# First weights split just before the first expert slot, and routing steps moved into the pauses of the slots

## The chip, the cores and the metric

The kernel runs on one core of a Trainium2 chip. Time is the device time of one execution in microseconds (us), median of several runs. The engines are TensorE (PE), VectorE (DVE), ScalarE (ACT), GpSimd (POOL) and SyncE (SP), which here only starts transfers. Each engine works through its own list of instructions in order; an instruction that waits for another engine or for a transfer holds up everything behind it in its list. PEld is the load of a stationary operand.

## The reference, cut to what matters

An attention over 32 memory rows per head, followed by a mixture of experts in which every token takes the one expert with the largest logit. Shapes: batch 8, heads 8, 576 positions of 64; so 4608 tokens of 512; 8 experts of 512 x 1024 and 1024 x 512. Everything is float32.

```python
a = softmax(phi, axis=2)                       # over the positions
k_m = einsum('bhsm,bhsd->bhmd', a, k)          # 32 memory rows per head
v_m = einsum('bhsm,bhsd->bhmd', a, v)
attn = softmax(q @ k_m.T / 8) @ v_m            # x: 4608 tokens of 512
logits = x @ w_gate;  e = argmax(logits)       # one expert per token
gate = softmax(logits)[e];  eom = sigmoid(x @ w_output_gate)[e]
out[token] = gate * eom * (relu(x[token] @ w1[e]) @ w2[e])
```

## The kernel before

**Attention.** The eight batches go in four pairs (`bp`), each pair in five units of queries, so 20 turns `t`, and three more turns until the last unit is through. One turn walks through the list `ORDER` of 16 letters; a letter's `LAG` says which unit it handles in turn `t`, unit `t - LAG`: `C` the scores, `S` shift by the maximum, `X` exponent on ACT, `D` divide, `B` transpose back, `V0` and `V1` the product with the memory values and its copy to `xo`, which is then stored to the table `xs` in DRAM. `M` and `m` advance the memory rows of later pairs. The instructions of each engine stand in the order in which this Python code emits them.

**Routing.** When a pair's last unit is stored, `rank(bp)` picks each token's expert from the logits, counts tokens per expert with matmuls against ones and a triangle (L246, L879 to L883, into the one bank `pr`), writes the gate values to `xs` and builds one-hot masks `Aw` on POOL. Beside it run the lists: `route_early(0)` after pair 1 makes list a (slots 0 and 1), `route_early(1)` after pair 2 list b (slots 2 to 4), `route_late` after pair 3 list l (all others). A list is a table of token numbers, made by a chain of small DVE operations and one group of matmuls (L227); `known` says that the experts of its slots are decided, `listed` that the token numbers are there. All of this is in generators that are advanced a few steps at a time, by the letters `R0`, `R1`, `R4` in the attention's turns.

**Expert slots.** A slot is up to 384 tokens (three blocks of 128) of one expert. POOL gathers the rows (`xg`, three buffers from turn 19 on), PE turns them (L991), ACT and DVE split them into a high and a low part (`xh`, `xl`), and three matmuls stand for one product of full precision. A slot's weights come in eight chunks `u`: SP loads a chunk (`w`, L508), ACT casts its high part (L519), DVE subtracts for the low part (L520). Chunks 0 to 3 give the hidden layer in groups of 12 matmuls of 384 columns (L1124), with `hh` on ACT and `hl` on DVE; chunks 4 to 7 give the output (L1143, 512 columns), which ACT scales and POOL scatters to `out`. The rows of the next slot are turned during chunks 4 to 7. There are 14 fixed slots and 22 spare ones behind branches.

**The seam.** Turns up to `t` = 19 (`START`), letter `S`, run alone; then slot 0 begins, and what is left of the attention is advanced in pauses of the slots: `hook()` is called 20 times in a slot of three blocks, after every group of 12 matmuls in chunks 0 to 3 and after every block in chunks 4 to 7. `hold(n)` lets a generator wait until `clock` has moved by `n` (by one at each letter of the attention, or at each pause once that is done); `take_pr()` waits until the bank `pr` has been read. `LATE` holds these numbers: `pe` ahead of routing matmuls, `dve` between them and their reader, `w` ahead of the first weight load, `lg` for the sum of the logits.

The lines on which the steps rest:

```python
elif w == "W":
    if order[0]["known"] and stream.parted < ring.size:
        stream.split(ring.size)
...
def hook():
    gathers(i)
    clock[0] += not att.gens
    (att if att.gens else late).step(HOOK[min(i, 5)])
```

`ring` (split chunks) has two buffers, four from turn 19 on; `raw` (loaded chunks) three, then five.

Of the kernel before, what the change touches and what calls it, by code (L numbers as in the profile page):

```python
# [19 lines left out]
NBP = B // 2  # L20
# [15 lines left out]
ORDER = ["R4", "W", "X", "S", "R0", "m", "D", "M", "B", "V0", "R1", "R1", "V1", "M", "m", "C"]  # L36
LAG = {"X": 1, "B": 2, "D": 1, "V": 3, "C": -1}
TICK = 0
HOOK = (2, 2, 2, 2, 2, 2)
START = 19  # L40
NKV = 8
NQ = 3
# [7 lines left out]
NPK = 1  # L50
PHI1 = 6
NEA = 3
LATE = {"lg": 8, "w": 2, "pe": 0, "dve": 0}
GROW = ((2, 2, 2), (6, 1, 0))
PUMP = (2, 1)
TURN = {3: (1, 4, 6, 9), 2: (1, 2, 4, 5)}
LAST = 1
# [8 lines left out]
def attention_moe(tc, phiT, kv, qT, wgo, wall, out):  # L66
# [3 lines left out]
    with contextlib.ExitStack() as ctx:  # L70
# [134 lines left out]
        def table(nm, q, nch, nblk):  # L205

            while nm == "l" and "rl" not in env:
                yield
            bw = (env["rl"] if nm == "l" else rt).tile([P, nch, 2, nblk], BF16, name="bw" + nm)
            w = min(nch, 9 * NBL // nblk // 9 * 9)  # L210
            for c in range(0, nch, w):
                b3 = [P, w, nblk]
                eq = rt.tile([P, 9 * NBL], BF16, name="eq")
                eq = eq[:, 0:w * nblk].rearrange("p (c b) -> p c b", c=w)
                V.tensor_tensor(eq, iota_blk[:, 0:nblk].unsqueeze(1).to_broadcast(b3),
                                q[:, c:c + w].unsqueeze(2).to_broadcast(b3), ALU.is_equal)
                yield
                for i in range(2):
                    V.tensor_tensor(bw[:, c:c + w, i], eq,
                                    tok_hl[:, i, c:c + w].unsqueeze(2).to_broadcast(b3), ALU.mult)  # L220
                yield
            yield
            yield from hold(LATE["pe"])
            yield from take_pr()
            pi = ps_r.tile([P, 2, NBL], F32, name="pr")
            for c in range(nch):
                T.matmul(pi[:, :, 0:nblk], Aw[:, c], bw[:, c], start=(c == 0), stop=(c == nch - 1))  # L227
            yield
            yield from hold(LATE["dve"])
            iv = rt.tile([P, NBL], F32, name="iv")  # L230
            i2 = rt.tile([P, NBL], F32, name="i2")
            ivv, i2v = iv[:, 0:nblk], i2[:, 0:nblk]
            V.tensor_copy(i2v, pi[:, 1, 0:nblk])
            yield
            V.scalar_tensor_tensor(ivv, pi[:, 0, 0:nblk], 64.0, i2v, ALU.mult, ALU.add)  # L235
            taken.clear()
            yield
            ig, io = idx[nm]
            V.tensor_scalar(ig[:], ivv, 1.0, 0.0, ALU.subtract, ALU.max)
            V.tensor_scalar(i2v, ivv, 0.0, 100000.0, ALU.is_equal, ALU.mult)  # L240
            yield
            V.scalar_tensor_tensor(io[:], ivv, -1.0, i2v, ALU.add, ALU.add)  # L242
# [6 lines left out]
        def route_early(k):  # L249

            nm, n, s0, nch = "ab"[k], NPS[k], sum(NPS[:k]), (k + 2) * NCH
            eo, en = epcs[k], epcs[k + 1]
            yield from hold(LATE["pe"])
            yield from take_pr()
            n_ = counts(k + 1)
            yield
            yield from hold(LATE["dve"])
            fi = rt.tile([P, 1, E], F32, name="fi")
            ge = triples(fi[:, 0], n_, thr_e)
            next(ge)  # L260
            taken.clear()
            yield
            yield from ge
            V.scalar_tensor_tensor(fi[:, 0], fi[:, 0], 3.0, eo[:], ALU.mult, ALU.subtract)
            yield
            inc = (yield from prefix(fi[:], 1))[:, 0]
            exc = rt.tile([P, E], F32, name="exc")
            ie = rt.tile([P, E], F32, name="ie")
            V.tensor_scalar(ie[:], inc, 3.0 * n, None, ALU.min)
            V.tensor_tensor(exc[:], inc, fi[:, 0], ALU.subtract)  # L270
            yield
            V.tensor_scalar(exc[:], exc[:], 3.0 * n, None, ALU.min)
            cle = count_le(slot[:, s0:s0 + n], iota_3[:, 0:n], n, ie[:])
            next(cle)
            yield
            next(cle)
            V.tensor_tensor(ie[:], ie[:], exc[:], ALU.subtract)
            yield
            last(cle)
            V.tensor_tensor(en[:], eo[:], ie[:], ALU.add)  # L280
            V.tensor_tensor(exc[:], exc[:], eo[:], ALU.subtract)
            known(*order[s0:s0 + n])
            yield
            if k == 0:
                yield from hold(LATE["w"])
                stream.fetch()
            t1, t2, t3 = yield from lookup(nch, exc[:], en[:], eo[:])
            while k + 1 not in ranked:
                yield
            j = jg[:, 0:nch]  # L290
            V.scalar_tensor_tensor(t1, t1, 1.0, j, ALU.add, ALU.add)
            V.tensor_tensor(t2, j, t2, ALU.is_lt)
            V.tensor_tensor(t3, j, t3, ALU.is_ge)
            yield
            V.tensor_tensor(t1, t1, t2, ALU.mult)
            yield
            V.tensor_tensor(t1, t1, t3, ALU.mult)
            yield
            yield from table(nm, t1, nch, 3 * n)
            for z in order[s0:s0 + n]:  # L300
                z["listed"] = True
            if k == 0:
                gathers(0)
            yield

        def route_late():
            yield from hold(LATE["pe"])
            yield from take_pr()
            n_ = counts(NBP - 1)
            yield  # L310
            yield from hold(LATE["dve"])
# [107 lines left out]
        env = {}  # L419
# [4 lines left out]
        def take_pr():  # L424

            while taken:
                yield
            taken.append(1)

        def hold(n):  # L430

            end = clock[0] + n
            while clock[0] < end:
                yield
# [23 lines left out]
        ring = Ring([P, 2, 1024], F32R, "whl")  # L458
# [16 lines left out]
        order = slots  # L475
# [354 lines left out]
        def rank(bp, lg):  # L830
# [41 lines left out]
            yield  # L872

            def rest():
                yield from hold(LATE["pe"])
                yield from take_pr()

                pr = ps_r.tile([P, NCH, E], F32, name="pr")
                T.matmul(pr[:], strict[:], oh, start=True, stop=False)  # L879
# [135 lines left out]
        def attention():  # L1015
# [8 lines left out]
            for t in range(NT + LAG["V"]):  # L1024
                for w in ORDER:
# [2 lines left out]
                        if w == "M" or t % 5 < 4:  # L1028
                            mem.step()
                    elif w[0] == "R":  # L1030
                        rou.step(int(w[1:]))
                    elif w == "W":
                        if order[0]["known"] and stream.parted < ring.size:
                            stream.split(ring.size)
                    elif w == "W":

                        while t == NT - 1 and stream.split(2):
# [175 lines left out]
        def run(st):  # L1213
# [8 lines left out]
            def hook():  # L1222
                gathers(i)
                clock[0] += not att.gens
                (att if att.gens else late).step(HOOK[min(i, 5)])

            for i in range(lo, hi):
                gathers(i, i + 1)
# [10 lines left out]
                    several(i, st, nxt, hook)  # L1239
                else:  # L1240
                    single(i, st, nxt)
                if i == LAST:
                    settle()

        pso.close()
        pso = contextlib.ExitStack()
        env["pd"] = pso.enter_context(tc.tile_pool(name="pd1", bufs=1, space=PSUM, reuse_waits="tile"))
        env["ps"] = pso.enter_context(tc.tile_pool(name="p0", bufs=5 - NPK, space=PSUM, reuse_waits="tile"))
        n = NPE + NPT + NPP
        run(stream)  # L1250
        used = nc.values_load(slot[0:1, NSLOT:], min_val=0, max_val=NSS)  # L1251
# [48 lines left out]
```

## Time and profile before

| | us |
|---|---|
| median of 3 runs (lowest, highest) | 617.65 (616.18, 618.13) |
| the profiled execution, its own time | 618.26 |
| its span in the trace | 616.6 |
| PE busy in the span | 541.8 (88%) |
| DVE, ACT, POOL busy | 344.2, 273.2, 160.1 |

Matmuls overlap, so a busy PE means that its list does not stand still. A timeline row gives start and length in us, engine, line and operation, output and inputs, shape and count, and in square brackets how long the engine stood idle before it and what ended that. A row of waits gives the total in us, how often, and the longest. A row of the windows view gives the stretch, its length, and for each of PE, PEld, DVE, ACT and POOL the busy time and the count, then PE's clock, the share of the transfers and GB/s.

### The profile page before, as it was taken

Reading aid. Unit: us, or ns where it says so; the run is one execution under the profiler, and the core shown is the slowest. Engines: PE = TensorE matmul, PEld = TensorE weight load, DVE = VectorE, ACT = ScalarE, POOL = GpSimd, SP = SyncE. Lnnn points to the kernel's source line nnn. Section 1 sums busy time; section 2 is a strip of 40 time slices with the busy share of each in tenths; the row PEclk is TensorE's granted clock in tenths of the full one; section 3 lists DMA queues with packets and bytes.
Section 4 is the critical chain, followed back from the end, with each engine's and each line's share of the span. In section 5 each row is a group of like instructions: output and inputs, shape, how many; then the busy total and the mean of one; then the engine's idle time right before and its main releaser. Section 6 shows DMA issues by size and latency. Waiting matters only on the chain. (4 is left out here: it accounts for less than half of the span.)

```text
span 616.6 us, 10779 instructions
## 1 busy us (share of the span) xinstructions
PE 541.8 (88%) x4107; PEld 467.0 (76%) x4107; DVE 344.2 (56%) x686; ACT 273.2 (44%) x456; POOL 160.1 (26%) x192
## 2 busy tenths in 40 slices
PE   4688777349999599989999999999999999999990
PEld 2355555239889489888998989898998989989970
DVE  3487989585655269975452635444453536556300
ACT  4475654424444146434444435344444436455310
POOL 2244466252410437012211303030201203210100
PEclk9779879659999799989999999999999999999995
DMA  8999999674555647855463755455554647673000
GB/s 305 412 368 389 406 366 335 224 231 126 170 164 167 204 110 258 312 168 161 153 195 120 228 154 195 137 173 175 158 175 133 193 154 227 200 238 114 27 5 25
DMA packets 41276, 124.13 MB, mean 201 GB/s; under 512 B 9408, under 2 KB 9472, under 8 KB 40832
## 3 DMA queue, kind: packets, MB, share of 16 engines
q1 hardware_dynamic: 35136, 102.71, 50.7%
q0 software_dynamic: 6080, 20.65, 9.5%
q8 instruction: 34, 0.56, 0.4%
q14 instruction: 26, 0.21, 0.1%
HBM read 102.99 MB, written 20.87 MB: 201 GB/s over the span
## 5 line engine op out<-in xcount | busy, mean ns | idle before, releaser
L1124 PE MATMUL bps<-xh,whl 128*128 128x384 f32 (+1 forms) x896 | 214.1, 322 | 0.0
L1143 PE MATMUL bps<-whl,hh 128*128 128x512 f32 x608 | 204.2, 401 | 0.0
L520 DVE TENSOR_TENSOR whl<-w,whl 128x1024 fp32r<-128x1024 f32 x112 | 137.0, 1230 | 76.3 <-ACT whl L519 76.2
L1124 PEld LDWEIGHTS bps<-xh,whl 128*128 128x128 f32 x896 | 157.2, 190 | 1.1 <-issue 0.2
L1124 PE MATMUL bps<-xl,whl 128*128 128x384 f32 (+1 forms) x448 | 143.9, 321 | 0.0
L1143 PEld LDWEIGHTS bps<-whl,hh 128*128 128x128 f32 x608 | 115.0, 189 | 23.4
L519 ACT CAST whl<-w 128x1024 fp32r<-128x1024 f32 x112 | 116.2, 1045 | 10.1 <-DMA w<-wall 8.1
L1143 PE MATMUL bps<-whl,hl 128*128 128x512 f32 x304 | 119.2, 392 | 0.0
L1129 ACT ACTIVATE hh<-bps 128x384 fp32r<-128x384 f32 (+1 forms) x96 | 48.9, 509 | 109.1 <-PE bps L1124 109.1
L1130 DVE SCALAR_TENSOR_TENSOR hl<-bps,hh 128x384 fp32r<-128x384 f32 (+1 forms) x96 | 55.4, 577 | 68.1 <-ACT hh L1129 68.0
L1124 PEld LDWEIGHTS bps<-xl,whl 128*128 128x128 f32 x448 | 85.3, 190 | 0.5
L1104 POOL DMA_INDIRECT out<-y,idx_ol x23 | 24.2, 1053 | 212.0 <-ACT y L1103 183.5
L993 DVE TENSOR_TENSOR xl<-bps,xh 128x384 fp32r<-128x384 f32 (+1 forms) x48 | 27.8, 578 | 69.1 <-ACT xh L992 68.9
L1143 PEld LDWEIGHTS bps<-whl,hl 128*128 128x128 f32 x304 | 57.7, 190 | 10.4
L992 ACT CAST xh<-bps 128x384 fp32r<-128x384 f32 (+1 forms) x48 | 23.8, 496 | 77.6 <-PE bps L991 77.6
L1103 ACT ACTIVATE y<-bps,xg 128x512 f32<-128x512 f32 x38 | 26.2, 688 | 66.5 <-PE bps L1143 23.7
L991 PE MATMUL bps<-ident,xg 128*128 128x128 f32 x152 | 26.2, 289 | 8.4 <-DMA xg<-xs,idx_gb 6.5
L481 POOL DMA_INDIRECT xg<-xs,idx_gl x23 | 28.2, 1226 | 20.9 <-DVE idx_ol L242 14.1
L826 PE MATMUL bpd<-ve_b,aT 64*128 64x144 f32 (+1 forms) x320 | 29.8, 340 | 3.6 <-DVE iv L235 2.3
L828 ACT COPY xo<-bpd 128x576 f32<-128x576 f32 x36 | 22.3, 638 | 22.1 <-PE bpd L826 9.4
L991 PEld LDWEIGHTS bps<-ident,xg 128*128 128x128 f32 x152 | 20.4, 148 | 15.3 <-issue 6.7
L793 POOL TENSOR_TENSOR ea<-ea,mx 128x512 f32<-128x512 f32 (+1 forms) x20 | 19.2, 959 | 48.6 <-DVE mx L791 48.6
(232 smaller groups left out, 435.5 us busy)
## 6 DMA issues: line engine op xcount, KB each, us to landing
w<-wall SPq DMA_DIRECT2D x112, 512.0 KB, 3.6
kvt<-kv SPq DMA_DIRECT2D x32, 512.0 KB, 8.2
xs<-xo SPq DMA_DIRECT2D x16, 576.0 KB, 5.5
qt<-qT SPq DMA_DIRECT2D x16, 512.0 KB, 9.1
ph<-phiT SPq DMA_DIRECT2D x3, 1152.0 KB, 12.5
kv<-kv SPq DMA_DIRECT2D x4, 512.0 KB, 10.4
ph<-phiT SPq DMA_DIRECT2D x4, 288.0 KB, 3.7
xs<-xo SPq DMA_DIRECT2D x8, 144.0 KB, 3.9
```

The costliest lines, as they stand in the source:

```text
L481: G.indirect_dma_start(out=z["xg"][:, k], out_offset=None, in_=xs[0:z["rows"]], in_offset=bass.IndirectOffsetOnAxis(ap=z["idx"][0][:, q:q ...
L519: A.copy(hl[:, 0], w[:])
L520: V.tensor_tensor(hl[:, 1], w[:], hl[:, 0].bitcast(F32), ALU.subtract)
L826: T.matmul(px[to:to + n, r, sl], z["aT"][h, o:o + n], ves[2 * bp + b][h, g], start=True, stop=True)
L991: T.transpose(pt[:, j, k * P:(k + 1) * P], xg[:, k, o:o + P], ident[:])
L993: V.tensor_tensor(xl[:, c:c + w, 0:n], pt[:, :, 0:n], xh[:, c:c + w, 0:n].bitcast(F32), ALU.subtract)
L1103: A.activation(y[:], py, AF.Copy, scale=z["xg"][:, k, P:P + 1])
L1104: G.indirect_dma_start(out=out, out_offset=bass.IndirectOffsetOnAxis(ap=z["idx"][1][:, z["q0"] + k:z["q0"] + k + 1], axis=0), in_=y[:], in ...
L1124: T.matmul(pb[:, j % pb.shape[1], 0:n_], w[:, b, o:o + P], x[a][:, cc, 0:n_], start=(n == 0), stop=(n == 11))
L1129: A.activation(h_[:, js, 0:n_], pb[:, :, 0:n_], AF.Relu)
L1130: V.scalar_tensor_tensor(l_[:, js, 0:n_], pb[:, :, 0:n_], 0.0, h_[:, js, 0:n_].bitcast(F32), ALU.max, ALU.subtract)
L1143: T.matmul(py[k], h[u - 4][a][:, f, k * P:(k + 1) * P], w[:, b, DM * f:DM * f + DM], start=(u == 4 and f == 0 and n == 0), stop=(u == 7 an ...
```

## The change

Four edits. The letter `W` no longer splits a chunk as soon as slot 0's expert is known; its second branch, so far never reached, now splits two chunks in turn 19, just ahead of slot 0. The letters `R` do nothing once three pairs have been stored, so that the third pair's `rank` and `route_early(1)` do not start before slot 0. In every pause of a slot the attention takes three letters where it took two, and the routing takes two steps of its own. `hold` waits only once the slots have begun (`env["open"]`), with `pe` 3 and `dve` 2 in place of 0 and 0, and stands behind `take_pr()`, where it stood ahead of it. `settle()`, which frees the attention's memory for more weight buffers, may come after the first slot if the attention is done by then; the order of the built program shows it after slot 1, as before.

```diff
-HOOK = (2, 2, 2, 2, 2, 2)
+HOOK = (3, 2)
...
-LATE = {"lg": 8, "w": 2, "pe": 0, "dve": 0}
+LATE = {"lg": 8, "w": 2, "pe": 3, "dve": 2}
...
             yield
+            yield from take_pr()
             yield from hold(LATE["pe"])
-            yield from take_pr()
             pi = ps_r.tile([P, 2, NBL], F32, name="pr")
...
         def hold(n):
 
+            if "open" not in env:
+                return
             end = clock[0] + n
...
                     elif w[0] == "R":
-                        rou.step(int(w[1:]))
-                    elif w == "W":
-                        if order[0]["known"] and stream.parted < ring.size:
-                            stream.split(ring.size)
+
+                        if len(left) < NBP - 1:
+                            rou.step(int(w[1:]))
                     elif w == "W":
 
                         while t == NT - 1 and stream.split(2):
                             pass
...
                 clock[0] += not att.gens
-                (att if att.gens else late).step(HOOK[min(i, 5)])
+                att.step(HOOK[0])
+                (rou if rou.gens else late).step(HOOK[1])
...
-                if i == LAST:
+                if "hs" not in env and (i == LAST or not att.gens):
                     settle()
...
+        env["open"] = True
         n = NPE + NPT + NPP
         run(stream)
```

The same exchange of `take_pr` and `hold` is made in `route_early`, `route_late` and `rank`. In the changed kernel lines behind L432 stand two to three numbers higher.

**ACT, where slot 0's expert becomes known** (`whl` is a split chunk, `ea` the scores, `kvm` the memory rows, `kT` and `vT_b` their transposes). Before:

```order
L797 ACTIVATE ea<-ea 128x256
L828 COPY xo<-bpd 128x576 x2
L519 CAST whl<-w 128x1024
L797 ACTIVATE ea<-ea 128x512
L706 ACTIVATE kvm<-pk,rs 128x128 x2
L720 COPY kT_198<-bpa 64x128 x2
L721 COPY vT_b<-bpa 64x256
```

Now:

```order
L799 ACTIVATE ea<-ea 128x256
L830 COPY xo<-bpd 128x576 x2
L799 ACTIVATE ea<-ea 128x512
L708 ACTIVATE kvm<-pk,rs 128x128 x2
L722 COPY kT_198<-bpa 64x128 x2
L723 COPY vT_b<-bpa 64x256
```

The first cast is gone from here, and with it the first subtraction from DVE; both stand, with a second chunk, directly ahead of slot 0. On SP the slot number is read, and three chunks are loaded, ahead of the store of `xo` and the load of queries behind which they stood.

**DVE, the last instructions ahead of slot 0** (`ohg`, `oc`, `ohc`, `zs`, `gd` belong to the third `rank`, `tge` and `fi` to list b, `xl` to slot 0's rows). Before:

```order
L813 STREAM_TRANSPOSE aT<-ea 128x512
L861 TENSOR_TENSOR ohg<-desc,pm 128x72
L863 TENSOR_REDUCE oc<-ohg 128x8
L864 TENSOR_TENSOR w__1909<-ohg,lg 128x72
L868 TENSOR_TENSOR ohc_90<-ohc_89,oc 128x8
L871 TENSOR_REDUCE zs<-w__1909 128x9
L184 TENSOR_TENSOR tge<-pr,thr_e 128x104
L186 TENSOR_REDUCE fi<-tge 128x8
L885 TENSOR_REDUCE gd<-w__1908 128x9
L520 TENSOR_TENSOR whl<-w,whl 128x1024
L788 STREAM_TRANSPOSE ea<-bpd 128x256
```

Now:

```order
L815 STREAM_TRANSPOSE aT<-ea 128x512
L522 TENSOR_TENSOR whl<-w,whl 128x1024 x2
L790 STREAM_TRANSPOSE ea<-bpd 128x256
L793 TENSOR_REDUCE mx<-ea 128x8
L947 TENSOR_REDUCE lg<-xo 128x32
L995 TENSOR_TENSOR xl<-bps,xh 128x384 x4
```

The steps of the third rank, and PE's counting matmuls L246 to L883 with them, have moved into slot 0, where L246 now stands between two groups of 12 expert matmuls and L881 (L879 before) two groups later; two subtractions stand where one stood.

**DVE, the end of list b** (`idx_gb` and `idx_ob` are its token numbers, `hl` a group of slot 1's hidden layer). Before, the rows at the end of that layer, with the turned rows of slot 2 (`xl`) behind them:

```order
L1130 SCALAR_TENSOR_TENSOR hl<-bps,hh 128x384 x2
L520 TENSOR_TENSOR whl<-w,whl 128x1024
L239 TENSOR_SCALAR idx_gb<-iv 128x9
L240 TENSOR_SCALAR i_2573<-iv 128x9
L242 SCALAR_TENSOR_TENSOR idx_ob<-iv,i_2573 128x9
L993 TENSOR_TENSOR xl<-bps,xh 128x384
```

Now, at the end of slot 0, with the first `hl` of slot 1 behind them:

```order
L995 TENSOR_TENSOR xl<-bps,xh 128x384
L239 TENSOR_SCALAR idx_gb<-iv 128x9
L240 TENSOR_SCALAR i_2489<-iv 128x9
L242 SCALAR_TENSOR_TENSOR idx_ob<-iv,i_2489 128x9
L522 TENSOR_TENSOR whl<-w,whl 128x1024
L1131 SCALAR_TENSOR_TENSOR hl<-bps,hh 128x384
```

List b stands a whole hidden layer (eight groups of 12 matmuls) earlier against the matmuls of slot 1.

More of the change, by code (lines that the diff above doesn't have):

```diff
@@ L252, in route_early @@
             eo, en = epcs[k], epcs[k + 1]
+            yield from take_pr()
             yield from hold(LATE["pe"])
-            yield from take_pr()
             n_ = counts(k + 1)
@@ L306, in route_late @@
         def route_late():
+            yield from take_pr()
             yield from hold(LATE["pe"])
-            yield from take_pr()
             n_ = counts(NBP - 1)
@@ L874, in rest @@
             def rest():
+                yield from take_pr()
                 yield from hold(LATE["pe"])
-                yield from take_pr()
                 pr = ps_r.tile([P, NCH, E], F32, name="pr")
```

## The prediction

> **What bounds the kernel now.** I read the page's forty slices first, then all waits of TensorE (PE), then the timelines of the engines around the longest ones.
>
> ```profile
> PE   4688777349999599989999999999999999999990
> ```
>
> From slice 9 on PE is full, except for the 5 in slice 13. Slices 7 and 8, about 108 to 139 us, are nearly empty: there attention ends and the expert slots begin. So time is to be had only before slot 0 starts and in that one later hole. The longest waits of PE in the whole span that the change can touch (us in total, times, longest):
>
> ```profile
> PE bpa L715 <- ACT kvm L706: 13.0, 3, 9.2
> PE bps L991 <- DMA xg<-xs,idx_gb: 6.5, 3, 6.0
> PE pr L227 <- DVE bwl L219: 2.3, 2, 1.5
> ```
>
> The 9.2 is one stall of PE, seen on PE and then on ScalarE (ACT):
>
> ```profile
> 115.55 0.73 PE L715 MATMUL bpa<-ident,kvm 128*128 128x128 f32 x2 [9.16 <-ACT kvm L706]
> ```
> ```profile
> 105.03 1.18 ACT L828 COPY xo<-bpd 128x576 f32<-128x576 f32 x2 [3.27 <-DMA xs<-xo]
> 113.66 1.04 ACT L519 CAST whl<-w 128x1024 fp32r<-128x1024 f32 x1 [7.45 <-DMA w<-wall]
> 114.61 0.62 ACT L797 ACTIVATE ea<-ea 128x512 f32<-128x512 f32 x1
> ```
>
> ACT is free at 106.21, but its next instruction is the cast of the first weights, whose transfer is still under way. The softmax exponent and the copies of kvm, whose data were there, stand behind it. PE's order then waits for ACT.
>
> **The lead-in, term by term.** The change takes this cast, and the next two, out of the attention turns. With it gone the exponent (L797) can start when POOL has its input ready:
>
> ```profile
> 105.62 1.04 POOL L793 TENSOR_TENSOR ea<-ea,mx 128x512 f32<-128x512 f32 x1
> ```
>
> That is at 106.7, 7.9 us earlier than 114.61. VectorE (DVE) gains less:
>
> ```profile
> 109.06 0.18 DVE L295 TENSOR_TENSOR q<-q,q 128x18 f32<-128x18 f32 x1
> 115.88 0.71 DVE L788 STREAM_TRANSPOSE ea<-bpd 128x512 f32<-128x512 f32 x1
> 121.48 1.22 DVE L520 TENSOR_TENSOR whl<-w,whl 128x1024 fp32r<-128x1024 f32 x1
> 126.22 0.56 DVE L239 TENSOR_SCALAR idx_ga<-iv 128x6 int32<-128x6 f32 x1
> 127.05 0.23 DVE L852 TENSOR_REDUCE lm<-lg 128x9 f32<-128x72 f32 x1
> 130.43 0.65 DVE L813 STREAM_TRANSPOSE aT<-ea 128x512 f32<-128x512 f32 x1
> 131.01 2.37 DVE L861 TENSOR_TENSOR ohg<-desc,pm 128x72 bf16<-128x72 f32 x1
> 135.30 1.23 DVE L520 TENSOR_TENSOR whl<-w,whl 128x1024 fp32r<-128x1024 f32 x1 [0.44 <-ACT whl L519]
> 136.44 0.44 DVE L788 STREAM_TRANSPOSE ea<-bpd 128x256 f32<-128x256 f32 x1
> ```
>
> After L295 ends at 109.24 DVE has one more small step (L297, 0.13) and then the transpose of 115.88: at 109.4, so 6.5 us earlier. From there DVE's own work sets the pace. The subtraction at 121.48 goes (1.1 to the next start): 7.6. The four rank steps that fill 127.05 to 128.00 go: 8.6. Then, from 131.01 to 136.44, DVE spends 5.4 us on the next rank steps and one subtraction; now two subtractions of 1.15 each stand there, 2.3, which by itself makes 11.7. But these two need their casts, and the casts stand on ACT behind the last two copies of xo:
>
> ```profile
> 128.30 1.33 PE L826 MATMUL bpd<-ve_b,aT 64*128 64x144 f32 x8 [0.78 <-ACT xo L828]
> 133.96 0.17 PE L246 MATMUL pr<-ohc,ones_b 128*128 128x8 bf16 x1 [3.72 <-DVE ohc L868]
> 136.94 2.82 PE L991 MATMUL bps<-ident,xg 128*128 128x128 f32 x12 [1.93 <-DVE ea L788]
> ```
> ```profile
> 131.31 0.26 ACT L865 ACTIVATE w__1908<-w__1908 128x72 f32<-128x72 f32 x1 [3.06 <-POOL w__1908 L855]
> 131.48 0.62 ACT L828 COPY xo<-bpd 128x576 f32<-128x576 f32 x1
> ```
>
> The copy at 131.48 waited for the rank exponent before it, not for PE, which was done at 129.63. Without that exponent it ends at 130.3 in the old count; that chain runs 7.7 to 7.9 earlier, so at 122.5. Two casts of 1.0 end at 124.5, the second subtraction at 126.0, the short transpose at 126.5, and slot 0's transposes (old start 136.94, 0.06 behind that transpose) begin at 126.6: **−10.3**. The gathered rows must be there too:
>
> ```profile
> 127.07 1.25 POOL L481 DMA_INDIRECT xg<-xs,idx_ga  x1 [0.32 <-DMA xs<-xo]
> 201.23 1.05 POOL L481 DMA_INDIRECT xg<-xs,idx_gb  x1 [17.14 <-DVE idx_ob L242]
> ```
>
> List a (L239, 126.22) moves up by 7.6, so the gather goes out at about 119.3. For slot 2 PE had all three blocks 7.1 us after the first issue (201.23, third block at 208.33, quoted below): 126.4. Both estimates agree. Bounds: −6.5, if nothing but the shift of 115.88 survives, and −11.7 by DVE alone.
>
> **The later hole.** PE's timeline:
>
> ```profile
> 200.53 0.39 PE L1143 MATMUL bps<-whl,hh 128*128 128x512 f32 x1
> 206.94 0.45 PE L991 MATMUL bps<-ident,xg 128*128 128x128 f32 x1 [6.03 <-DMA xg<-xs,idx_gb]
> 208.33 0.47 PE L991 MATMUL bps<-ident,xg 128*128 128x128 f32 x1 [0.27 <-DMA xg<-xs,idx_gb]
> 208.46 0.78 PE L1143 MATMUL bps<-whl,hh 128*128 128x512 f32 x1
> 211.86 0.63 PE L1143 MATMUL bps<-whl,hh 128*128 128x512 f32 x2
> 213.94 0.39 PE L1143 MATMUL bps<-whl,hh 128*128 128x512 f32 x1
> 214.17 0.49 PE L991 MATMUL bps<-ident,xg 128*128 128x128 f32 x3
> 214.41 0.47 PE L1143 MATMUL bps<-whl,hh 128*128 128x512 f32 x1
> ```
>
> List b ends on DVE only at 201, its gather goes out at 201.23, and slot 2's transposes, in slot 1's second half, stand waiting. Nine matmuls from 211.86 to 213.94 give a pitch of 0.231. Without the hole three transposes (0.24, from 214.17 to 214.41) would follow 200.53 + 0.23 and the next matmul would stand at 201.0, not at 208.46: 7.45. The 18 matmuls from 208.46 to 214.17 took 5.71 instead of 18 × 0.231 = 4.16, since PE's clock was down after the stop: 1.55. Together 9.0. In the change list b ends on DVE before slot 1's first hl, eight groups of 2.08 us (the length of one is shown below) ahead of its use, and the gather needs some 7. The whole hole goes: **−9.0**. Bounds: 0, if the list is late again, and −9.0.
>
> List l's matmuls waited 2.3 us for bwl just after its last product was made. They now stand three pauses, half a weight chunk of PE work each, behind it: **−2.0**, between 0 and −2.3.
>
> **What is added.** The counting matmuls of the third rank (L246 to L883, 0.17 + about 0.5 beside 133.96) stood in idle time and now stand in slot 0: **+0.9** with their weight loads. In slot 0 PE also waits for DVE at them:
>
> ```profile
> 142.04 0.49 ACT L1129 ACTIVATE hh<-bps 128x384 fp32r<-128x384 f32 x1 [1.76 <-PE bps L1124]
> 144.12 0.49 ACT L1129 ACTIVATE hh<-bps 128x384 fp32r<-128x384 f32 x1 [1.59 <-PE bps L1124]
> ```
> ```profile
> 134.16 0.27 DVE L184 TENSOR_TENSOR tge<-pr,thr_e 128x104 f32<-128x104 f32 x1
> ```
>
> Twelve expert matmuls take 2.08 us (142.04 to 144.12). L881 reuses the bank that L184 reads, one such group after L246's pause. But between the group's end and L184 stand hh (0.49), a cast (1.04), a subtraction (1.23), a reduction and L184 (0.27): some 3.5, so PE waits 1.4. Behind the waiting L881 stand only expert matmuls. At L246 the same count (two casts and two subtractions fall in the first pause) gives 1.0, and the copies of xo behind casts 0.4: **+2.8**. Bounds: 0, if DVE catches up, and 8. DVE was busy
>
> ```profile
> 137.00:179.00 42.00, 42.00 (x234) 36.70 (x235) 27.09 (x72) 19.04 (x31) 12.39 (x16) 0.96 0.56 169
> ```
>
> 27 of 42 us there (third busy number), and takes over about 9 us of rank and list steps: 36 of some 45, so it is late at single places and no bound of the slot. The transfer of the first weights costs nothing: the first was in at 113.66, later ones at most a few us after it, and slot 0 now starts at 126.6.
>
> **Sum:** −10.3 − 9.0 − 2.0 + 0.9 + 2.8 = −17.6. The profiled execution took 618.26 (span 616.6), 0.6 above the median of 617.65; it gives 600.7, and against the median **600 us**. PE is full from the hole to the end of the last fixed slot, so what is gained there reaches the end.
>
> **Rivals.**
>
> *A store takes the cast's place.* SyncE now reads the slot and issues three weight loads ahead of the store of 106.23, which goes out 3 us later:
>
> ```profile
> 95.20 0.38 SPq L937 DMA_DIRECT2D xs<-xo  x1
> ...
> 106.23 0.36 SPq L937 DMA_DIRECT2D xs<-xo  x1
> ```
>
> The copy of xo two turns on needs that buffer. If the store took as long as the one that ACT waited for at 105.03 (issued 95.20: 9.8 us), it would land at 119.3, while the copy would be ready at 115.3: 4 us lost on ACT and PE alike, 604. With 3 more of stalls in slot 0 it is 607. For it: three weight loads of 512 KB now go out just ahead of the store. Against: the wait at 105.03 is ACT's only one of its kind between 90 and 140 us. Chance 0.18.
>
> *The hole stays.* Ranking the third pair starts later than before, so list b could come late and slot 2 wait again: 600 + 9 = 609. Against it stands DVE's order. Chance 0.08.
>
> *DVE pays for POOL, and slots 0 and 1 stall: slower.* POOL's masks now stand beside the expert work of both slots:
>
> ```profile
> L911 POOL TENSOR_SCALAR Aw<-iota_row,row 128x128 bf16<-128x128 bf16 x18 | 15.6, 880 | 9.1 <-DVE row L901 9.0
> ```
>
> If DVE stood still during all 18 masks and PE with it, that is 15.6 us, and with the upper bound of the stalls (5.2 more) 621. It decides once DVE's slack in slot 0, 45 − 36 = 9, is used up. Against: these 18 ran in expert slots before too, where PE never waited for hl. [...] Chance 0.05. *No change* would need gain and stalls to cancel by accident: 0.03.
>
> **How the numbers follow.** My own case, 595.5 to 604, has 0.66, the store 0.18, the hole 0.08, no change 0.03, slower 0.05. The low end takes all low bounds: −11.7 − 9.0 − 2.3 + 0.9 = −22.1, so 595.5. The high end, 609, takes in the store with its stalls and the remaining hole. A measurement of this kernel tells 0.3%, 1.9 us, from no change: faster 0.92, same 0.03, slower 0.05.
>
> **What would show it.** On ACT no cast before slot 0 but two in a row behind the xo copies, each without a wait for w; the first L993 row at 125 to 128 us and its wait by DVE's ea or by xg; the transposes of slot 2 without a wait for idx_gb; short waits of PE at L246 and L881 inside slot 0. Wrong would be a long wait of ACT for xs<-xo near 115, a wait of slot 2 for its gather, or PE waiting over 8 us for DVE in slots 0 and 1.

## The result, and the profile after

The changed kernel took **607.81 us** (median; 607.07 to 609.62) against 617.89 (616.18 to 618.62) for the kernel before on the same chip: a ratio of 0.9845, 95% interval 0.9815 to 0.9875. That is 10.1 us faster. The forecast was 600 with a range of 595.5 to 609, so the time lies in the range, at its slow end: of the 17.6 us that the sum promised, 7 did not come. This part finds them.

TensorE's (PE) busy tenths and granted clock in forty slices, from the page of the kernel after:

```profile
PE   3578888558997999899999999999999999999990
PEclk9987788759999999999999999999999999999996
```

The hole in slice 13 is now a 9. Slices are counted from 0, each 15.15 us long. The thin place ahead of slot 0 is left (slices 7 and 8, 106 to 136 us, a 5 each), and a slight dip near 190 (slice 12) is new. PE's waits in the kernel after, in the columns that the prediction used:

```profile
PE pr L246 <- DVE ohc L870: 4.8, 3, 3.2
...
PE bpa L717 <- ACT kvm L708: 3.0, 3, 1.9
PE pr L227 <- DVE bwl L219: 2.6, 2, 1.5
PE pr L227 <- DVE bwa L219: 2.4, 1, 2.4
```

The 9.2 us stall behind the cast is gone (13.0 for kvm is now 3.0), and so is the wait of slot 2 for its gather. The wait for bwl, which was to go, is still there: 2.6 against 2.3. A single wait of 3.2 at L246 is new.

To see where each gain went I compared the starts of the same expert matmuls in the two profiled executions (spans 616.6 and 606.0):

| stretch | before | after | difference | forecast |
|---|---|---|---|---|
| span's start to slot 0's first hidden matmul | 139.42 | 131.50 | −7.9 | −10.3 |
| from there to slot 1's first output matmul | 58.57 | 67.00 | **+8.4** | +3.7 |
| slot 1's output half | 27.68 | 18.43 | −9.25 | −9.0 |
| slot 2, and slot 3's hidden half | 56.99 | 55.70 | −1.3 | −2.0 |
| the rest | 333.94 | 333.37 | −0.6 | 0 |
| sum | 616.6 | 606.0 | −10.6 | −17.6 |

So the hole did what was forecast. The lead-in lacks 2.4, the stretch through slots 0 and 1 costs 4.7 more, the wait for bwl lacks 0.7.

**The lead-in.** PE's timeline of the kernel after:

```profile
120.32 0.68 PE L782 MATMUL bpd<-qt,kT 64*32 64x64 f32 x32
126.81 0.69 PE L993 MATMUL bps<-ident,xg 128*128 128x128 f32 x2 [5.81 <-DVE ea L790]
129.45 2.40 PE L993 MATMUL bps<-ident,xg 128*128 128x128 f32 x10 [1.95 <-DMA xg<-xs,idx_ga]
131.50 0.67 PE L1125 MATMUL bps<-xh,whl 128*128 128x384 f32 x1
```

The transposes begin at 126.81; the forecast had 126.6. But then they stop for the third gathered block until 129.45. ACT, DVE and POOL just before:

```profile
120.98 1.99 ACT L521 CAST whl<-w 128x1024 fp32r<-128x1024 f32 x2
```
```profile
122.06 4.34 DVE L522 TENSOR_TENSOR whl<-w,whl 128x1024 fp32r<-128x1024 f32 x2 [0.67 <-issue]
126.32 0.44 DVE L790 STREAM_TRANSPOSE ea<-bpd 128x256 f32<-128x256 f32 x1
```
```profile
118.23 1.24 POOL L483 DMA_INDIRECT xg<-xs,idx_ga  x1 [0.32 <-DVE idx_oa L242]
...
121.09 1.00 POOL L483 DMA_INDIRECT xg<-xs,idx_ga  x1 [0.30 <-DVE sa L809]
122.12 1.06 POOL L795 TENSOR_TENSOR ea<-ea,mx 128x512 f32<-128x512 f32 x1
123.12 1.05 POOL L810 TENSOR_TENSOR ea<-ea,sa 128x512 f32<-128x512 f32 x1
```

PE waited 5.81 us for a transpose on DVE (L790) that stood behind the two subtractions. These took 4.34 us instead of the 2.3 in the sum: the first 3.21, beside two POOL operations of 1.06 and 1.05, and the second 1.21. And the third block was there 8.4 us after its issue began (121.09 to 129.45).

**Slot 1.** Three engines around 190 us in the kernel after, POOL, ScalarE (ACT) and DVE:

```profile
183.91 1.09 POOL L483 DMA_INDIRECT xg<-xs,idx_gb  x1 [0.30 <-issue]
...
190.55 1.00 POOL L483 DMA_INDIRECT xg<-xs,idx_gb  x1 [0.30 <-issue]
191.56 0.33 POOL L857 TENSOR_TENSOR w__2570<-lg,lm 128x72 f32<-128x72 f32 x1
```
```profile
183.44 0.49 ACT L1130 ACTIVATE hh<-bps 128x384 fp32r<-128x384 f32 x1 [0.65 <-PE bps L1125]
191.93 0.26 ACT L867 ACTIVATE w__2570<-w__2570 128x72 f32<-128x72 f32 x1 [7.99 <-issue]
192.09 0.47 ACT L1130 ACTIVATE hh<-bps 128x384 fp32r<-128x384 f32 x1
```
```profile
192.60 0.56 DVE L1131 SCALAR_TENSOR_TENSOR hl<-bps,hh 128x384 fp32r<-128x384 f32 x1 [7.02 <-issue]
194.68 0.16 DVE L870 TENSOR_TENSOR ohc<-ohc,oc 128x8 bf16<-128x8 bf16 x1
```

The last pair's rank now stands in slot 1's hidden half. Its subtraction L857 is a third of a microsecond on POOL, but six gather issues of slots 2 and 3 (list b, 1.3 us apart) stand ahead of it. ACT's exponent L867 waits for it, 7.99 us. Behind that exponent stands the expert's own hh, behind hh DVE's hl, behind that ohc, and PE's counting matmul L246 waits for ohc. PE, in the kernel after:

```profile
145.93 0.17 PE L246 MATMUL pr<-ohc,ones_b 128*128 128x8 bf16 x1 [0.77 <-DVE ohc L870]
...
151.52 0.21 PE L881 MATMUL pr<-ohg,strict 128*128 128x72 bf16 x1 [1.15 <-DVE tge L184]
...
194.89 0.17 PE L246 MATMUL pr<-ohc,ones_b 128*128 128x8 bf16 x1 [3.16 <-DVE ohc L870]
```

The first two rows are the waits in slot 0 that the prediction named, the third is the new one. The twelve hidden matmuls that follow it, up to the start of the output half at 198.50, took 3.6 us instead of 2.08, at a low granted clock (stretch, length, PE busy with its count, granted clock, DMA share, GB/s):

```profile
194.89:198.50 3.61, 3.61 (x14) 0.57 0.68 168
```

The pause cost 3.16 and the slow restart 1.5, 4.7 in all. That is the size of what the second row of the table lacks.

### The profile page after: what moved, and what is told of

The parts are those of the page before. It is cut to its first block, busy times and chain, and to the rows that moved or that the text cites. A ratio compares the mean times of both kernels' runs of the same rounds, so it can differ in the third digit from the quotient of the medians.

```text
span 606.0 us, 10785 instructions
## 1 busy us (share of the span) xinstructions
PE 541.7 (89%) x4107; PEld 467.0 (77%) x4107; DVE 341.1 (56%) x686; ACT 273.0 (45%) x456; POOL 157.7 (26%) x192
## 5 line engine op out<-in xcount | busy, mean ns | idle before, releaser
L828 PE MATMUL bpd<-ve_b,aT 64*128 64x144 f32 (+1 forms) x320 | 30.0, 346 | 3.3 <-DVE aT L815 1.7
L1105 POOL DMA_INDIRECT out<-y,idx_ob x9 | 10.8, 1196 | 80.8 <-ACT y L1104 70.9
L913 POOL TENSOR_SCALAR Aw<-iota_row,row 128x128 bf16<-128x128 bf16 x36 | 23.5, 668 | 28.5 <-DVE row L903 28.4
```

The source lines that it names most:

```text
L828: T.matmul(px[to:to + n, r, sl], z["aT"][h, o:o + n], ves[2 * bp + b][h, g], start=True, stop=True)
L1105: G.indirect_dma_start(out=out, out_offset=bass.IndirectOffsetOnAxis(ap=z["idx"][1][:, z["q0"] + k:z["q0"] + k + 1], axis=0), in_=y[:], in ...
```

## The experiments

Two theories were open for each loss. For slot 1: POOL's queue (one late operation), or simply too much ranking for DVE and ACT beside slot 1. For the lead-in: weight loads that share the DMA engines with the gather, or DVE's subtractions that hold up the gather or the last scores. First, what the two parts of the change do alone.

**w_only.** The kernel before without the early split:

```diff
-                    elif w == "W":
-                        if order[0]["known"] and stream.parted < ring.size:
-                            stream.split(ring.size)
```

> The kernel before, with the first part of the change alone: no first weights split in attention's W place before the last round; the order of the routing's steps is the old one. If the change's two parts are separate, the lead-in is some 8 us shorter (slot 0's hidden matmuls start near 131.5 instead of 139.4 us), the idle stretch ahead of slot 2's hidden matmuls stays (9 us), and the median is 609.5 to 611 us. If the lead-in also needs the routing's rest ahead of the first slot (DVE's and POOL's steps of the routing in the way of the last scores), the lead-in gains 4 us or less and the median is 613 to 616 us. If the idle stretch ahead of slot 2 takes the gain up, because its list is due no earlier, the median stays at 616 to 618 us.

Measured: 611.75 us (610.11 to 612.13), ratio 0.9919 (0.9893 to 0.9944). PE in this kernel:

```profile
129.91 2.82 PE L991 MATMUL bps<-ident,xg 128*128 128x128 f32 x12 [3.06 <-DVE ea L788]
```
```profile
PE bps L991 <- DMA xg<-xs,idx_gb: 6.2, 3, 5.6
```

The first kind of outcome: the lead-in gains 7.0 alone (slot 0's first hidden matmul at 132.38), slots 0 and 1 keep their old lengths, and slot 2 still waits for its gather. The median is 0.8 us above the range given.

**routing_only.** The kernel after with those three lines put back.

> The changed kernel with the old first split put back: the first weights are split as soon as slot 0 is known, in attention's W place; the routing rests and steps as in the changed kernel. If the parts are separate, slot 0's hidden matmuls start near 139 us again and the idle stretch ahead of slot 2 stays away: 614 to 616 us, since the stall in slot 1 (4.6 us) and the cold start come with this part. If the routing's rest alone frees the last scores, slot 0 starts at 132 to 135 us and the time is 608 to 611 us.

Measured: 614.77 us (612.35 to 616.77), ratio 0.9962 (0.9944 to 0.9981). ACT's timeline and PE's waits:

```profile
110.35 1.04 ACT L521 CAST whl<-w 128x1024 fp32r<-128x1024 f32 x1 [4.92 <-DMA w<-wall]
```
```profile
PE bpa L717 <- ACT kvm L708: 10.5, 3, 6.6
...
PE pr L246 <- DVE ohc L870: 4.9, 3, 3.4
```

The cast is back, and PE stands 6.6 us behind it; the stall in slot 1 (3.4) comes with the routing part. Slot 0's first hidden matmul stands at 137.0, where the expectation had about 139. Slot 1's output half took 18.3 us, so the hole is gone here as well. The parts are nearly separate: 5.7 and 2.7 us of gain alone (each against 617.43, the kernel before on their chip), 10.1 together, 1.7 more than their sum. The routing part removes a hole of 9 us and gives most of it back in slots 0 and 1.

**sub_dve.** The kernel after, the last pair's subtraction moved off POOL:

```diff
-            G.tensor_tensor(w2_[:], lt, lmb, ALU.subtract)
+            (V if bp == NBP - 1 else G).tensor_tensor(w2_[:], lt, lmb, ALU.subtract)
```

> The changed kernel, with one operation elsewhere: the subtraction w2_ = lt - lm of the last pair's rank (L857) goes to DVE instead of POOL. Theory one, POOL's queue: in the changed kernel that subtraction stood behind six gather issues on POOL (183.91 to 191.55 us), ACT's exponent waited 7.99 us for it, and slot 1's hidden matmuls stood 3.16 us at L246 and then ran slowly; with it on DVE, ACT's exponent has its input some 7 us earlier, the wait of 3.16 us at L246 falls under 0.5 us, slot 1's output half starts about 4 us earlier, and the median falls from 607.8 to 603.0 to 604.5 us. Theory two, the last pair's ranking is simply too much work for DVE and ACT beside slot 1: DVE has one operation of some 0.2 us more, the wait at L246 stays above 2 us, and the time stays at 607 to 609 us.

Measured: 604.58 us (603.66 to 606.92), ratio 0.9815 (0.9786 to 0.9844). DVE and ACT in this kernel:

```profile
183.27 0.23 DVE L857 TENSOR_TENSOR w__2570<-lg,lm 128x72 f32<-128x72 f32 x1
```
```profile
184.73 0.25 ACT L867 ACTIVATE w__2570<-w__2570 128x72 f32<-128x72 f32 x1
```

The exponent has no wait, and PE has no wait left in slot 1's hidden half: it took 16.79 us instead of 21.52. So it was POOL's queue, as theory one says; the median stands 0.1 above its range. With the stall gone, the second stretch of the table is 61.81 us, 3.2 longer than before; the forecast had 3.7 (what the 3.2 is made of stands further below).

The kernel after and its variants start attention's last scores anywhere from 120.3 to 123.0 us in their single profiled executions, though little of what comes ahead of them differs. So for the following ones I also count from the start of the last scores' matmuls (the row at 120.32 above) to slot 0's first hidden matmul, and to the end of the span:

| kernel | median us | last scores at | to slot 0's first hidden matmul | to the end of the span |
|---|---|---|---|---|
| before | 617.89 | 129.56 | 9.86 | 487.0 |
| after | 607.81 | 120.32 | 11.18 | 485.7 |
| sub_dve | 604.58 | 121.71 | 11.15 | 481.2 |
| loads_held | 606.70 | 121.20 | 8.96 | 483.7 |
| split_after_s | 609.42 | 120.69 | 11.11 | 486.8 |
| all3 | 603.59 | 120.97 | 8.46 | 480.3 |
| all3_warm | 601.32 | 121.89 | 7.95 | 477.9 |
| all3_hold | 598.68 | 122.95 | 8.56 | 476.5 |
| sub_hold | 601.63 | 120.69 | 10.48 | 479.2 |
| all5 | 597.18 | 121.19 | 7.81 | 474.3 |

**loads_held.** The weight loads after the first two splits wait for slot 0's rows:

```diff
-            def fetch(self):
+            def fetch(self, after=None):
+                if "held" in env:
+                    return
...
+                    if after is not None:
+                        A.copy(w[0:1, 0:1], after)
...
-                        while t == NT - 1 and stream.split(2):
-                            pass
+                        if t == NT - 1:
+                            env["held"] = True
+                            while stream.split(2):
+                                pass
...
                         turn_x(order[i], c)
+                    if env.pop("held", None):
+                        st.fetch(order[i]["xg"][0:1, 2, 0:1])
```

> The changed kernel, in which the weight loads that followed the first two splits (four of 512 KB each from 121.74 us) are sent only after slot 0's gathered rows have landed (ACT writes one element of each load's target from the last gathered block, so the load waits for it). Theory one, the loads take the gather's queues: the third gathered block, which landed about 129.4 us, 8.3 us after its issue began, lands 4.5 to 6 us after it, slot 0's transposes end 2.5 to 3.5 us earlier, and the median is 604 to 606 us. Theory two, DVE's two subtractions and POOL's two operations on ea (122.06 to 126.4 us) hold the gather or the last scores up: the third block still lands 7.5 us or more after its issue, slot 0's start stays within 0.5 us, and the time stays at 607 to 609 us, or rises by what slot 0 then waits for weights.

Measured: 606.70 us (606.55 to 608.13), ratio 0.9842 (0.9815 to 0.9869). POOL's third issue and PE:

```profile
121.97 0.99 POOL L483 DMA_INDIRECT xg<-xs,idx_ga  x1 [0.31 <-DVE sa L813]
```
```profile
127.69 2.82 PE L997 MATMUL bps<-ident,xg 128*128 128x128 f32 x12 [5.81 <-DVE ea L794]
```

PE takes all twelve transposes at once: the third block is there at most 5.7 us after its issue began, not 8.4. The wait of 5.81 for L790 (L794 here) is untouched. The windows of the kernel after and of this one (length, PE busy, granted clock, DMA share, GB/s) show the other transfers:

```profile
124.00:127.00 3.00, 0.19 (x1) 0.50 1.01 310
127.00:129.50 2.50, 0.56 (x3) 0.50 1.00 381
```
```profile
125.00:127.70 2.70, 0.01 (x1) 0.50 0.47 153
```

In the kernel after all DMA engines were full while the third block was due; here they were half empty. DVE's two subtractions still stood ahead of L794, and PE's transposes began 6.49 us behind the start of the last scores in both kernels (127.69 here, 126.81 there), so the subtractions were not what held the block back. The mechanism of theory one holds. The gain in time is not clear of the noise: 2.0 us counted from the last scores in one execution each, 1.1 by the medians, next to nothing by the ratios to the kernel before (0.9842 and 0.9845); the median stands 0.7 above theory one's range.

**split_after_s.** The two splits behind the last scores' step (S) instead of ahead of it (in W):

```diff
-
-                        while t == NT - 1 and stream.split(2):
-                            pass
+                        pass
...
                         shift(st[g])
+                        while t == NT - 1 and stream.split(2):
+                            pass
```

> The changed kernel, in which the two splits ahead of slot 0 stand behind the step that takes attention's last scores (L790) on ACT and DVE, not ahead of it. In the changed kernel PE stood 5.81 us behind that L790, which waited on DVE for the two subtractions of 4.34 us, and then 1.95 us for the gathered rows. Theory one, two limits in a row (L790 behind the subtractions, then the gather): the wait for L790 goes, the gather then sets the start alone at 10 to 11 us behind the start of the last scores' end, and the time moves by less than 1 us: 606.5 to 608. Theory two, DVE's subtractions of two SBUF inputs also slow the gather (they started at 122.06, between its third issue and its landing): with them 1 to 2 us earlier or later nothing lands sooner, and the subtraction still takes over 4 us for the two. Theory three, L790 was the whole loss: slot 0 starts 2.5 us or more earlier and the time falls to 604 to 605.5.

Measured: 609.42 us (607.41 to 610.53), ratio 0.9864 (0.9833 to 0.9895). PE and DVE:

```profile
129.75 2.40 PE L993 MATMUL bps<-ident,xg 128*128 128x128 f32 x10 [4.73 <-DMA xg<-xs,idx_ga]
```
```profile
121.86 0.45 DVE L790 STREAM_TRANSPOSE ea<-bpd 128x256 f32<-128x256 f32 x1
125.16 2.36 DVE L522 TENSOR_TENSOR whl<-w,whl 128x1024 fp32r<-128x1024 f32 x2 [2.40 <-DMA xs<-xo]
```

L790 comes 4.5 us sooner and the wait for it is gone, but PE then waits 4.73 for the third block, until 129.75, and slot 0 starts no sooner (11.11 against 11.18). Two limits in a row, as theory one says, though the median is 1.4 above its range. The subtractions took 2.36 us here, with no POOL operation on ea beside them, so they do not take over 4 us by themselves. They stood 3 us later and the third block was there 8.3 us after its issue began (121.46), against 8.4. With loads_held, theory two falls: the subtractions do not hold a gather that has been issued. An issue that is still to go out may suffer: the first of slot 1's, at 125.26 beside them, took 2.04 us, and 1.05 without them in the kernel after.

**all3.** The three edits together.

> The changed kernel with three edits at once: the last pair's subtraction on DVE (L857), the weight loads held until slot 0's rows have landed, and the two splits behind the last scores' step on DVE. If the two limits of the lead-in are the ones read from the traces, slot 0's hidden matmuls start 7.3 to 7.8 us behind the end of the last scores (10.5 in the changed kernel, 8.3 with the loads held alone), and the gain on the subtraction's move adds: 600.5 to 602.5 us. If the gather needs its 8 us from its last issue whatever DVE and the loads do, the start stays at 10 us behind and the time is that of the moved subtraction alone, 604 to 605.

Measured: 603.59 us (603.0 to 605.14), ratio 0.978 (0.9756 to 0.9805). POOL's first issue and PE:

```profile
118.88 1.24 POOL L483 DMA_INDIRECT xg<-xs,idx_ga  x1 [0.32 <-DVE idx_oa L242]
```
```profile
127.38 2.40 PE L997 MATMUL bps<-ident,xg 128*128 128x128 f32 x10 [2.05 <-DMA xg<-xs,idx_ga]
```

Slot 0 starts 8.46 behind the start of the last scores. That is neither theory's number, and the median lies between the two ranges given: the gather still is the last to come, 8.5 us after its first issue, so the 7.1 that slot 2's gather had taken was not to be had here. Of the 2.7 us gained over sub_dve at this point only 0.9 reach the end; 0.8 are lost again in slot 0's hidden half, whose first 13 matmuls took 3.78 us against 2.97 in sub_dve, and 1.2 to a slow clock in slot 3 (0.81 in the first 6.5 us of its hidden half, last section).

**all3_warm.** As all3, with PE kept busy in the pause:

```diff
+                        wm = ps_k.tile([P, 2, 2 * D], F32, name="pk")
+                        for _ in range(16):
+                            T.matmul(wm[:].rearrange("p g d -> p (g d)")[:, 0:P], ident[:], ident[:],
+                                     start=True, stop=True)
```

> The same three edits, and 16 matmuls of the identity into an unread PSUM tile between attention's last scores and slot 0's transposes, where PE stands idle (some 0.24 us each, 3.8 us in all). If the slow start of slot 0 is the granted clock of 0.50 that the idle time leaves behind, the clock is at 1.00 by the first hidden matmul, the first 24 hidden matmuls take 4.2 instead of 5.5 us, the transposes 1.4 to 2 instead of 2.8 us, and the time is 1 to 2.5 us under the three edits alone. If the clock follows something else (the whole core's load), nothing moves, or the 16 matmuls put slot 0 back by up to 2 us where they last beyond the wait.

Measured: 601.32 us (599.61 to 602.78), ratio 0.9735 (0.9712 to 0.9758). Windows of all3 and of this kernel, the last of each being the first 24 hidden matmuls:

```profile
127.38:129.43 2.05, 2.05 (x10) 0.50 0.48 133
129.43:134.60 5.17, 5.17 (x24) 0.70 0.84 247
```
```profile
122.50:127.60 5.10, 5.10 (x40) 0.70 0.81 259
127.60:129.84 2.24, 1.70 (x15) 1.00 0.29 62
129.84:134.20 4.36, 4.36 (x24) 1.00 0.87 283
```

The clock is at 1.00 from the transposes on, and the 24 matmuls take 0.8 us less. By the medians the gain is 2.3 us, as expected. In the two traces 1.8 of it stand in slot 0 (0.5 at its start, 1.3 in its hidden half).

**all3_hold.** As all3, with a longer hold:

```diff
-LATE = {"lg": 8, "w": 2, "pe": 3, "dve": 2}
+LATE = {"lg": 8, "w": 2, "pe": 6, "dve": 3}
```

> The same three edits, with the hold ahead of the routing's matmuls at 6 instead of 3 steps and ahead of its DVE reads of them at 3 instead of 2. If the waits of 0.77 us at L246 and 1.15 us at L881 (L885 here) in slot 0 are PE coming to these matmuls before DVE has their one-hots, they fall under 0.3 us each and the time is 1 to 1.9 us under the three edits alone. The rival: the later hold puts off the lists, the last one (which slot 2 waits for) above all, a wait for the gather or the weights of slot 1 or slot 2 comes back, and the time is 0 to 5 us above the three edits alone.

Measured: 598.68 us (597.13 to 601.5), ratio 0.9698 (0.9672 to 0.9724), 4.9 under all3 by the medians and 3.9 counted from the last scores. PE:

```profile
146.57 0.18 PE L246 MATMUL pr<-ohc,ones_b 128*128 128x8 bf16 x1
...
247.99 0.45 PE L1132 MATMUL bps<-xl,whl 128*128 128x384 f32 x1 [2.47 <-DVE xl L999]
```

In slot 0 neither L246 nor L885 waits any more. No list came late for its gather. The wait for bwl is gone too, but PE stands 2.47 us for xl in its place. The gain is more than the 1 to 1.9 expected, and the hold did not make all of it. Slot 0's hidden half is 3.45 us shorter than in all3: 1.9 are the two waits, 0.3 the counting matmuls from L885 on, which went into the slot's output half, and 1.3 the expert matmuls, which ran faster. Of these 1.3, 0.8 fall on the first 13, which are the same in both kernels but took 2.94 us here (131.51 to 134.45) and 3.78 in all3 (129.43 to 133.21).

**sub_hold** has only the moved subtraction and the longer hold.

> The changed kernel with two small edits: the last pair's subtraction on DVE (L857) and the hold at 6 and 3 steps instead of 3 and 2. The lead-in stays as in the changed kernel. If the two gains add (some 4.5 us from the subtraction, counted from the start of the last scores, and 1.9 us for the waits at L246 and L881, up to 3.9 as the three edits with the longer hold had it), the median is 600 to 602.5 us. If the longer hold helped only where slot 0 started sooner, it is 603 to 605 us.

Measured: 601.63 us (599.79 to 602.74), ratio 0.9731 (0.9702 to 0.976), in the range for two gains that add. Against sub_dve the longer hold is worth 3.0 us by the medians (on different chips) and 2.0 counted from the last scores.

**all5** has every edit that gained.

> All edits that gained, together: the last pair's subtraction on DVE, the weight loads held until slot 0's rows have landed, the splits behind the last scores' step on DVE, the 16 identity matmuls in PE's pause, and the longer hold. Over the three edits alone (603.6) the matmuls gave 2.3 us and the longer hold 4.9 by the medians, 2.4 and 3.9 us by the spans counted from the last scores' start. If they add, the median is 596 to 598 us, 3.2 to 3.5% under the kernel before; if both gains came from the granted clock in slot 0 and are partly the same, 598 to 600 us.

Measured: **597.18 us** (595.83 to 598.75) against 618.02, ratio 0.9669 (0.964 to 0.9698), in the range for gains that add. It beats the changed kernel by 10.6 us and the kernel before by 20.8.

## Why the prediction was right, and where its sum was not

**The range.** The direction was right, and the stall behind the cast and the hole went as described, but that the range held the time is partly luck. The prediction's own case ended at 604. What stretched the range to 609 were two rivals, the store in the cast's place and the hole that stays, and neither of them cost the time that is missing.

**The lead-in (−10.3; measured −7.9): the step that failed is the landing of the gather.** The prediction took 7.1 us from first issue to third block, from slot 2's gather, and got 126.4. It took 11.2 (118.23 to 129.45). loads_held and all3 show why: 2.7 us of it are the weight loads that the split itself sends (5.7 against 8.4 us from the third issue), and even without them it is 8.5, not 7.1; that last difference was not explained. That the first weights' transfer "costs nothing" was right for their arrival and wrong for what it takes from others. The other route to the same 126.6, through DVE, was met (126.81), by two errors that cancel: the casts came 1.5 us sooner than worked out (122.97 for 124.5), and the subtractions cost 4.34 for 2.3. The excess of 2.0 is about the 2.1 of the two POOL operations beside them, and all of it fell on the first subtraction. The trace of before already held such a case: the rank step L861 took 2.37 us at 131.01, beside the same two POOL operations (131.23 and 132.23), and 0.22 at its shortest elsewhere. The sum let these 2.37 go with the rank step; the loss stayed and fell on the subtraction that now stands there. Both POOL operations kept their length (1.06 and 1.05 us here, 1.05 each in split_after_s, where no subtraction stood beside them), so the whole delay fell on DVE.

**The hole (−9.0; measured −9.25)** went as forecast, and for the reason given: list b is ready in time, and slot 2's transposes do not wait. The first three in the kernel after:

```profile
201.43 0.49 PE L993 MATMUL bps<-ident,xg 128*128 128x128 f32 x3
```

**What is added (+3.7; measured +8.4): the step that failed is that only slot 0 was costed.** In slot 0 the waits at L246 and L881 are 0.77 and 1.15, 1.9 for 2.8, and sub_dve shows 3.2 for the whole. The 4.7 that are left came from the last pair's rank in slot 1. The prediction went through DVE's order and budget and did not follow this rank onto POOL, where one small operation met six gather issues.

That 3.2 lies near 3.7 is partly luck too. Counting each PE row up to the next one, less PE's idle time, the kernel after spends 5.1 of its 8.4 on the three waits, 0.3 on the counting matmuls (forecast 0.9), and the other 3.0 on the same expert matmuls running slower, a term that the sum did not have: 1.6 in slot 0's hidden half, 0.2 in its output half, 1.2 more than before in slot 1's hidden half. Attention's and list b's matmuls only change places between the two slots. PE came to slot 0 from the broken wait of the lead-in, and its first stretch there was slow, at a clock of 0.53; before, the first 2.6 us had a clock of 0.89:

```profile
131.50:134.10 2.60, 2.60 (x11) 0.53 0.85 290
```

**The wait for bwl (−2.0; measured −1.3, the wait itself not at all).** "Three pauses behind its last product" supposed that DVE makes the product when its turn comes in the program. DVE was behind, and its last products came only when PE stood there already:

```profile
254.41 1.07 DVE L219 TENSOR_TENSOR bwl<-eq,tok_hl 128x405 bf16<-128x405 bf16 x2
```

It ends at 255.48, and PE's row for it starts at 255.54. all3_hold moves the wait to xl and gains nothing there. The −1.3 that this stretch did gain is not the change's doing as far as the runs show: the waits are 0.3 longer, and slot 3's hidden matmuls took 16.7 us at a granted clock of 1.00 instead of 18.3, of which the 5.3 behind the waits (272.70 to 278.00) had 0.68, and this came and went among the kernels with the same waits (last section).

**The rivals.** *A store takes the cast's place* came true in its mechanism, and with it one of the signs that the prediction had named for being wrong, a long wait of ACT for xs<-xo near 115. ACT in the kernel after:

```profile
115.91 0.64 ACT L830 COPY xo<-bpd 128x576 f32<-128x576 f32 x1 [4.42 <-DMA xs<-xo]
116.44 0.63 ACT L799 ACTIVATE ea<-ea 128x512 f32<-128x512 f32 x1
```

Its price was not the 4 us supposed. The exponent behind the copy got its input from POOL only at 116.41 and started at 116.44, so the wait did not hold it up; around it PE's rows name DVE (2.42 at L227 for bwa, 1.74 at L828 for aT), and the last scores began 9.2 us sooner than before. No run takes this wait away. *The hole stays* did not come. *DVE pays for POOL* came for one subtraction, 2 us, far from the 15.6 that would have made the kernel slower. Those were the author's estimate from the masks, and beside masks the subtractions kept their length: 1.23 us at 161.41 and 1.24 at 212.41, with a median of 1.23 over all 112.

## What to carry to other kernels

When a step is moved, follow every one of its instructions onto its engine's queue and ask what stands ahead of it there: a third of a microsecond on POOL behind six gather issues cost 4.7 us on PE, three engines further on. A landing time taken from another stretch did not hold where the same change sent weight loads beside the gather: 7.1 us from first issue to third block there, 11.2 here, 8.5 in all3 with the loads held. And when two limits stand one behind the other, removing one of them may show nothing: the later splits were worth 0.1 us at slot 0's start alone and 0.5 on top of the held loads (2.2 alone, 2.7 together), by one execution each.

## What the runs showed of the hardware

The same pause of PE did not always cost the same. In slot 2's last stretch PE waits for bwl twice in many of these kernels, 1.1 and 1.5 us in the kernel after, 1.2 and 1.5 in split_after_s. Afterwards the clock stayed up in the one and fell in the other (the same columns as above):

```profile
256.00:262.00 6.00, 6.00 (x37) 1.00 0.69 210
```
```profile
256.00:262.00 6.00, 6.00 (x27) 0.72 0.65 210
```

Slot 3's hidden half took 16.7 us in the kernel after, sub_dve and loads_held, and 17.9 to 18.3 in routing_only, split_after_s, all3 and all3_warm, each in its one profiled execution and all with these two waits (1.03 to 1.18 and 1.53 us). Over its first 6 to 6.5 us the clock was 1.00 in the kernel after and in loads_held, 0.72 in split_after_s, 0.81 in all3 and 0.74 in all3_warm. The 1.6 between the kernel after and split_after_s is more than the 1.1 us by which split_after_s lies above the kernel after, counted from the last scores. So a difference of this size between two kernels needs a look at the clock before it gets a cause. What makes the clock fall after one such pause and not after another was not shown: nearly equal pauses, unequal clocks. In all3_warm matmuls whose result nobody reads filled the pause ahead of slot 0: over those 5.10 us the clock was 0.70 in the mean, and in the transposes behind them 1.00, where all3 had 0.50.
